# Loading V and V^T one tile pair sooner in a shared DMA queue, and spreading a refill over more steps

## The chip, the cores and the metric

The kernel runs on one core of a Trainium2 chip. The metric is device time in microseconds (us); a smaller one is better. A core has TensorE (PE in the profile; its weight loads are PEld), VectorE (DVE), ScalarE (ACT), GpSimd (POOL) and SyncE (SP), which here issues every DMA. The *granted clock* is the share of TensorE's full clock that its throttle let through (1.00 is all of it).

## The reference

Two independent attention blocks, A and B, forward and backward. For each block with 8 batches of 96 queries, 32 heads, 512 cached keys and a head size of 128:

```python
q = (x @ wq).reshape(B, Sq, H, Dh).transpose(0, 2, 1, 3)
scores = jnp.einsum("bhqd,bhkd->bhqk", q, k_cache) * (Dh ** -0.5)
p = softmax(scores)
o = jnp.einsum("bhqk,bhkd->bhqd", p, v_cache)
out = o.transpose(0, 2, 1, 3).reshape(B, Sq, H * Dh) @ wo
# and, by vjp of the whole with grad_out: dx, dk_cache, dv_cache, dwq, dwo
```

Inputs and outputs are bf16. What matters is the traffic: each cached K and V is read twice (plain, and transposed by the DMA), and each dK and dV is written once. One transfer moves two heads of one batch, 256 KB.

## The kernel before

All work is emitted in *steps* ("ticks"), one for each tile, a (head, batch). Each piece of a tile's work is placed at the tile's step plus an offset, then all pieces are sorted by step and slot. What SyncE issues follows that order strictly. Loads and stores serve a pair of heads, so one pair takes two steps.

```python
OFF = dict(kt=-3, vt=2, vn=1, kn=4, dv=7, dk=10, s2=3, s3=3, s4=4, s5=5, s6=6, s7=8, s8=9)
# kt, vt: transposed loads of K, V   kn, vn: plain loads   dv, dk: stores
# s2: S = Q K^T   s5: O = P V (needs V)   s6: dP = dO V^T (needs V^T)   s8: dQ = dS K (needs K)
...
def p_ldT(h, b, which):          # K^T (5 buffers) or V^T (4 buffers)
    ...
    t_ = kvp.tile([128, F4 * KC, 16], BF16, name=key + "_p", bufs=5 if which == 0 else 4)
    sp(nc.sync.dma_start_transpose(t_[:], src))
def p_ldn(h, b, which):          # K or V (4 buffers each)
    t_ = kvp.tile([128, HP, KC, 128], BF16, name=key, bufs=4)
    sp(nc.sync.dma_start(...))
...
# block B only: x and g are filled again while block A ends and B begins
for t in range(TT):                                   # TT = 6
    tt = tick0 - 11 + 5 * (t // 3)
    em.add(tt - 4, SL_LOAD + 0.5, setup_stage(t))     # staged g tile, in an "ob" buffer
    em.add(tt, SL_HEAD - 1, setup_T(1, t))            # its transposes on PE
for t in range(TT):
    em.add(tick0 + NG0 + t, SL_LOAD + 0.5, setup_nat(1, t, t + 1))       # g, NG0 = 15
    em.add(tick0 + NX0 + 2 * t, SL_LOAD + 0.6, setup_nat(0, t, t + 1))   # x, NX0 = 18
...
# for the first head of each pair, ct the step of the pair
em.add(ct + OFF["vt"], SLOTS["LOAD"], p_ldT(h, b, 1))
em.add(ct + OFF["vn"], SLOTS["LOAD"] + 0.1, p_ldn(h, b, 1))
em.add(ct + OFF["kn"], SLOTS["LOAD"] + 0.1, p_ldn(h, b, 0))
em.add(ct + OFF["dv"], SLOTS["LOAD"] + 0.2, p_st(h, b, 1))
em.add(ct + OFF["dk"], SLOTS["LOAD"] + 0.2, p_st(h, b, 0))
```

Of the kernel before, what the change touches and what calls it, by code (L numbers as in the profile page):

```python
# [30 lines left out]
SL_LOAD = 0  # L31
# [9 lines left out]
SL_GRP = 95  # L41
SL_SETUP = 96

OFF = dict(kt=-3, vt=2, vn=1, kn=4, dv=7, dk=10, s2=3, s3=3, s4=4, s5=5, s6=6, s7=8, s8=9)
HP = 2
HK = [
    dict(pA=-12, pB=-7, pC0=[-6, -4], pC1=[-5, -3], pD1=-2, pD0=0, qA0=21, qA1=25, qB=[28, 25]),
# [7 lines left out]
GT0, NG0, NX0 = 0, 15, 18  # L55
# [4 lines left out]
SLOTS = dict(LOAD=0, S2A=5, S2B=5.5, S7=10, S8=20, S6=25, S5=30, S4=40, S3A=52, S3B=53, S5B=54, HEAD=SL_HEAD, GRP=SL_GRP)  # L60
# [17 lines left out]
def build_block(tc, em, tick0, blk, x, kc, vc, wq, wo, g_all, out_all, dx, dk, dv, dwq, dwo, ident, ones, pools, HG=4, first=True, groups=None):  # L78
# [51 lines left out]
    def setup_nat(which_, t0_, t1_):  # L130
        def f():
            key, _, src_flat = KEYS[which_]
            if t0_ == 0:
                S[key] = const.tile([128, TT, D], BF16, name=key, bufs=1)
            sp(nc.sync.dma_start(S[key][:, t0_:t1_, :], src_flat[t0_ * 128:t1_ * 128, :].rearrange("(t p) d -> p t d", p=128)))
        return f

    def setup_stage(t):
        def f():
            S[("g_nat", t)] = wk.tile([128, D], BF16, name="ob", bufs=4)  # L140
            sp(nc.sync.dma_start(S[("g_nat", t)][:], g_flat[t * 128:(t + 1) * 128, :]))
        return f

    def setup_xT(c):
        def f():
            if c == 0:
                S["xT"] = const.tile([128, DC, T], BF16, name="xT", bufs=1)
            sp(nc.sync.dma_start_transpose(S["xT"][:, c, :], x_flat[:, c * 128:(c + 1) * 128]))
        return f
# [27 lines left out]
    if first:  # L177
        for t in range(TT):
            late = t * 128 >= tsplits[0][1]
            em.add(tick0 - 15, SL_LOAD + (2 if late else 0), setup_nat(0, t, t + 1))  # L180
            em.add(tick0 - (7 if late else 9), SL_HEAD, setup_T(0, t))
            em.add(tick0 + GT0, SL_LOAD - 2, setup_nat(1, t, t + 1))
            em.add(tick0 + GT0, SL_HEAD + (2 if late else -1), setup_T(1, t))
    else:
        for c in range(DC):
            em.add(tick0 - 17 + (3 * c) // 2, SL_LOAD + 0.5, setup_xT(c))
        for t in range(TT):
            tt = tick0 - 11 + 5 * (t // 3)
            em.add(tt - 4, SL_LOAD + 0.5, setup_stage(t))
            em.add(tt, SL_HEAD - 1, setup_T(1, t))  # L190
        for t in range(TT):
            em.add(tick0 + NG0 + t, SL_LOAD + 0.5, setup_nat(1, t, t + 1))
            em.add(tick0 + NX0 + 2 * t, SL_LOAD + 0.6, setup_nat(0, t, t + 1))

    def pA_wq(h):
        def f():
# [75 lines left out]
    def p_ldT(h, b, which):  # L272
        def f():
            key = "KT" if which == 0 else "VT"
            t_ = kvp.tile([128, F4 * KC, 16], BF16, name=key + "_p", bufs=5 if which == 0 else 4)
            src = (kc if which == 0 else vc)[b, h:h + HP].rearrange("h (r f) d -> (h r) (f d)", r=R8)
            sp(nc.sync.dma_start_transpose(t_[:], src))
            for j in range(HP):
                half = t_[:, :, j * R8:(j + 1) * R8]
                CS.setdefault((blk, h + j, b), {})[key] = half.rearrange("p (f c) r -> p f c r", c=KC)  # L280
        return f

    def p_ldn(h, b, which):
        def f():
            key = "K_sb" if which == 0 else "V_sb"
            t_ = kvp.tile([128, HP, KC, 128], BF16, name=key, bufs=4)
            src = (kc if which == 0 else vc)[b, h:h + HP]
            sp(nc.sync.dma_start(t_[:].rearrange("p h c d -> p h (c d)"), src.rearrange("h (p c) d -> p h (c d)", c=KC)))
            for j in range(HP):
                CS[(blk, h + j, b)][key] = t_[:, j]  # L290
        return f
# [229 lines left out]
    def gW(g):  # L521
        def f():
            if g == 0:
                setup_acc()
        return f
# [32 lines left out]
    for g in range(NG):  # L558
        h0 = GH0[g]
        for hh in range(groups[g]):  # L560
            h = h0 + hh
            j = h % HP
            c0t = tick0 + (h - j) * B
            hk = (HKE if first and h >= H - HP else HK if h >= HP else HK1 if first else HK2)[j]
            early = first and h < HP
            soon = 2 if first and HP <= h < 2 * HP and j == 0 else 0
            if j == 0:
                em.add(tick0 - 15 if early else c0t + hk["pA"] + soon, SL_LOAD + (1 if early else 0), pA_wq(h))
            em.add(tick0 + GT0 if early else c0t + hk["pA"] + soon, SL_LOAD - 1 if early else SL_LOAD, pA(h))
            em.add(c0t + hk["pB"], SL_HEAD, pB(h))  # L570
            em.add(c0t + OFF["s5"], SL_LOAD, h_alloc(h))
            for si in range(NTS):
                em.add(c0t + hk["pC0"][min(si, len(hk["pC0"]) - 1)], SL_HEAD, pC(h, 0, si))
                em.add(c0t + hk["pC1"][min(si, len(hk["pC1"]) - 1)], SL_HEAD, pC(h, 1, si))
            em.add(c0t + hk["pD1"], SL_HEAD, pD(h, 1))
            em.add(c0t + hk["pD0"], SL_HEAD, pD(h, 0))
            for b in range(B):
                ct = c0t + b * HP + j
                if j == 0:
                    em.add(tick0 - 13 if early and b == 0 else ct + (max(OFF["kt"], -1) if early else OFF["kt"]), SLOTS["LOAD"], p_ldT(h, b, 0))  # L580
                    em.add(ct + OFF["vt"], SLOTS["LOAD"], p_ldT(h, b, 1))
                    em.add(ct + OFF["vn"], SLOTS["LOAD"] + 0.1, p_ldn(h, b, 1))
                    em.add(ct + OFF["kn"], SLOTS["LOAD"] + 0.1, p_ldn(h, b, 0))
                    em.add(ct + OFF["dv"], SLOTS["LOAD"] + 0.2, p_st(h, b, 1))
                    em.add(ct + OFF["dk"], SLOTS["LOAD"] + 0.2, p_st(h, b, 0))
                em.add(ct + OFF["s2"], SLOTS["S2A"], c_s2a(h, b))
                em.add(ct + OFF["s2"], SLOTS["S2B"], c_s2b(h, b))
                em.add(ct + OFF["s3"], SLOTS["S3A"], c_s3a(h, b))
                em.add(ct + OFF["s3"], SLOTS["S3B"], c_s3b(h, b))
                em.add(ct + OFF["s5"], SLOTS["S5B"], c_s5b(h, b))  # L590
                em.add(ct + OFF["s4"], SLOTS["S4"], c_s4(h, b))
                S45.setdefault(ct + OFF["s5"], [None, None, None])[0] = (blk, h, b)
                S45.setdefault(ct + OFF["s4"], [None, None, None])[1] = (blk, h, b)
                S45.setdefault(ct + OFF["s6"], [None, None, None])[2] = (blk, h, b)
                S78.setdefault(ct + OFF["s8"], [None, None])[0] = (blk, h, b)
                S78.setdefault(ct + OFF["s7"], [None, None])[1] = (blk, h, b)
                em.add(ct + OFF["s6"], SLOTS["S6"], c_s6(h, b))
                em.add(ct + OFF["s7"], SLOTS["S7"], c_s7(h, b))
            em.add(c0t + hk["qA0"], SL_HEAD, qA(h, 0))
            for di in range(len(dsplits)):  # L600
                em.add(c0t + hk["qB"][min(di, len(hk["qB"]) - 1)], SL_HEAD + 1, qB(h, di))
            em.add(c0t + max(hk["qB"]) + (1 if first and h >= H - 3 * HP else 2), SL_LOAD + 0.3, qB_st(h))
            em.add(c0t + hk["qA1"], SL_HEAD, qA(h, 1))
            if j == HP - 1:
                for (k_, c_lo, c_hi) in hk["qD"]:
                    em.add(c0t + k_, SL_HEAD + 2, qD(h - j, c_lo, min(c_hi, DC)))
                em.add(c0t + k_ + 2, SL_LOAD + 0.3, qD_st(h - j))
        cLg = tick0 + (h0 + groups[g]) * B - 1
        gs0 = max(3, (GSPREAD0 * groups[g]) // HG)
        gs1 = max(3, (GSPREAD1 * groups[g]) // HG)  # L610
        em.add(cLg + OFF["s5"] - 2, SL_LOAD, gW(g))
        subs = [(t, di) for t in range(TT) for di in range(len(dsplits))]
        n = len(subs)
        for which in (0, 1):
            for i, (t, di) in enumerate(subs):
                if which == 0:
                    tk = cLg + OFF["s5"] + 2 + (i * gs0) // n
                else:
                    tk = cLg + OFF["s8"] + 2 + gs0 - 3 + (i * gs1) // n
                em.add(tk, SL_GRP, gU(g, which, t, di))  # L620
                if g == NG - 1 and di == len(dsplits) - 1:
                    em.add(tk + 2, SL_LOAD + 0.3, gU_st(g, which, t))
# [124 lines left out]
```

## Time and profile before

| kernel before | |
|---|---|
| time, median of 3 runs | 1647.15 us (1645.1 to 1650.86) |
| profiled execution | 1644.9 us, granted clock 0.998 |
| PE idle in it | 44.2 us (an upper bound, see the result) |
| DMA queue | 454.57 MB, packets' time 103.3% of 16 engines (the packets' times are added up, so this can pass 100%) |

The prediction shows the busy line, the waits and the stages. Here is one more place, the worst in block A. It is the timeline of PE in the kernel before; columns are start, duration, engine, source line, operation, output and inputs, count, and in brackets the idle time just before and what ended it:

```profile
69.62 0.42 PE L411 MATMUL dP_ps<-VT_p,dOT_h 128*96 128x512 bf16 x1 [2.28 <-DMA VT_p<-in_A_v_cache_dram]
...
71.66 0.34 PE L430 MATMUL dq_dst_ps<-dST_sb,K_sb 128*128 128x96 bf16 x4 [0.59 <-DMA K_sb<-in_A_k_cache_dram]
...
74.08 0.50 PE L362 MATMUL optp_ps<-PT_sb,V_sb 128*128 128x96 bf16 x4 [1.41 <-DMA V_sb<-in_A_v_cache_dram]
```

### The profile page before, as it was taken

Reading aid. Unit: us, or ns where it says so; the run is one execution under the profiler, and the core shown is the slowest. Engines: PE = TensorE matmul, PEld = TensorE weight load, DVE = VectorE, ACT = ScalarE, POOL = GpSimd, SP = SyncE. Lnnn points to the kernel's source line nnn. Section 1 sums busy time; section 2 is a strip of 40 time slices with the busy share of each in tenths; the row PEclk is TensorE's granted clock in tenths of the full one; section 3 lists DMA queues with packets and bytes.
Section 4 is the critical chain, followed back from the end, with each engine's and each line's share of the span. In section 5 each row is a group of like instructions: output and inputs, shape, how many; then the busy total and the mean of one; then the engine's idle time right before and its main releaser. Section 6 shows DMA issues by size and latency. Waiting matters only on the chain.

```text
span 1644.9 us, 55391 instructions
## 1 busy us (share of the span) xinstructions
PE 1600.7 (97%) x20713; PEld 1260.4 (77%) x20906; DVE 1340.4 (81%) x3406; ACT 1349.3 (82%) x3498; POOL 533.3 (32%) x1026
## 2 busy tenths in 40 slices
PE   8899999999999999999899999999999999999998
PEld 6777877777777787777777777777787777878776
DVE  5786888888888888878778778888888888888796
ACT  6888988889788798888868889788798888879783
POOL 1333333333333333333323333333333333333331
PEclk9999999999999999999999999999999999999999
DMA  9999999999999999999999999999999999999995
GB/s 263 250 279 283 275 275 288 266 280 287 284 281 288 293 266 287 267 289 270 287 282 297 291 284 288 286 283 291 278 290 273 289 277 297 279 295 271 279 279 170
DMA packets 375566, 458.12 MB, mean 279 GB/s; under 512 B 40704, under 2 KB 367104, under 8 KB 367104
## 3 DMA queue, kind: packets, MB, share of 16 engines
q1 hardware_dynamic: 375296, 454.57, 103.3%
q8 instruction: 163, 2.67, 0.7%
q14 instruction: 107, 0.88, 0.1%
HBM read 160.10 MB, written 159.12 MB: 194 GB/s over the span
## 4 chain that ended last, share of the span: by engine, by line
PE 88%; DMA 6%; ACT 2%; DVE 2%; issue 1%; POOL 0%; SPq 0%; DVEq 0%; ACTq 0%
PE o_ps L536 12%; PE q_ps L250 12%; PE dwq_ps L511 6%; PE dV_ps L387 6%; PE dK_ps L453 6%; PE S_ps L314 6%; PE dwo_ps L491 6%; PE dP_ps L411 6%; PE optp_ps L362 6%; PE optp_ps L369 5%; PE dq_dst_ps L430 5%; PE dq_dst_ps L437 5%; PE n_ps L265 3%; PE nat_ps L477 3%; DMA V_sb<-in_A_v_cache_dram 2%; DMA V_sb<-in_B_v_cache_dram 1%
## 5 line engine op out<-in xcount | busy, mean ns | idle before, releaser
L401 POOL TENSOR_TENSOR prod<-OT_h,dOT_h 128x96 bf16<-128x96 bf16 x512 | 187.4, 366 | 836.0 <-DVE rinv L336 463.3
L346 POOL TENSOR_SCALAR P_sb<-E_sb,rinv 96x512 bf16<-96x512 bf16 x508 | 350.8, 691 | 244.6 <-DVE rinv L336 244.4
L458 ACT ACTIVATE dK_sb<-dK_ps 128x512 bf16<-128x512 f32 x512 | 305.8, 597 | 137.9 <-PE dK_ps L453 135.0
L326 ACT ACTIVATE E_sb<-S_ps,negm 96x512 bf16<-96x512 f32 x512 | 351.9, 687 | 67.0 <-DVE negm L316 53.7
L316 DVE TENSOR_REDUCE negm<-S_ps 96x1 f32<-96x512 f32 x512 | 347.5, 679 | 67.9 <-PE S_ps L314 67.2
L415 DVE SCALAR_TENSOR_TENSOR dS_sb<-dP_ps,dl_ps,P_sb 96x512 bf16<-96x512 f32 x512 | 380.3, 743 | 4.0 <-PE dl_ps L413 3.8
L392 ACT ACTIVATE dV_sb<-dV_ps 128x512 bf16<-128x512 f32 x512 | 307.8, 601 | 12.4 <-PE dV_ps L387 11.0
L376 ACT ACTIVATE PT_sb<-optp_ps 128x384 bf16<-128x384 bf16 x512 | 255.7, 499 | 5.6 <-DVE OT_h L373 4.7
L439 DVE COPY dST_sb<-dq_dst_ps 128x384 bf16<-128x384 bf16 x512 | 177.3, 346 | 50.7 <-PE dq_dst_ps L437 49.2
L411 PE MATMUL dP_ps<-VT_p,dOT_h 128*96 128x512 bf16 x512 | 195.9, 383 | 7.0 <-DMA VT_p<-in_A_v_cache_dram 3.9
L387 PE MATMUL dV_ps<-dOnat_h,P_sb 96*128 96x128 bf16 x2048 | 199.7, 219 | 2.1 <-DVE ob L546 1.7
L453 PE MATMUL dK_ps<-Qnat_h,dS_sb 96*128 96x128 bf16 x2048 | 198.9, 219 | 0.1
L314 PE MATMUL S_ps<-KT_p,QT_h 128*96 128x512 bf16 x512 | 194.0, 379 | 0.3
L453 PEld LDWEIGHTS <-dS_sb 96*128 96x128 bf16 x2048 | 147.5, 97 | 48.0
L362 PE MATMUL optp_ps<-PT_sb,V_sb 128*128 128x96 bf16 x2048 | 169.6, 204 | 10.2 <-DMA V_sb<-in_A_v_cache_dram 5.8
L369 PE MATMUL optp_ps<-ident,P_sb 96*128 96x96 bf16 x2048 | 172.4, 206 | 2.3 <-DVE P_sb L346 1.6
L430 PE MATMUL dq_dst_ps<-dST_sb,K_sb 128*128 128x96 bf16 x2048 | 171.8, 205 | 0.8 <-DMA K_sb<-in_A_k_cache_dram 0.6
L437 PE MATMUL dq_dst_ps<-ident,dS_sb 96*128 96x96 bf16 x2048 | 171.7, 205 | 0.0
L362 PEld LDWEIGHTS <-V_sb 128*128 128x128 bf16 x2048 | 107.0, 96 | 58.8 <-DMA V_sb<-in_A_v_cache_dram 7.9
L536 PE MATMUL o_ps<-wo_r,OT_h 128*128 128x128 bf16 (+1 forms) x722 | 144.5, 294 | 2.4
L536 PE MATMUL o_ps<-wqT_h,dQT_h 128*128 128x512 bf16 (+1 forms) x720 | 144.2, 294 | 2.5
L373 DVE CAST OT_h<-optp_ps 128x96 bf16<-128x96 f32 x512 | 125.0, 244 | 10.9 <-PE optp_ps L369 10.0
(75 smaller groups left out, 3047.4 us busy)
## 6 DMA issues: line engine op xcount, KB each, us to landing
out_dram<-dV_sb SPq DMA_DIRECT2D x256, 256.0 KB, 4.5
out_dram<-dK_sb SPq DMA_DIRECT2D x256, 256.0 KB, 4.4
V_sb<-in_A_v_cache_dram SPq DMA_DIRECT2D x128, 256.0 KB, 4.3
K_sb<-in_A_k_cache_dram SPq DMA_DIRECT2D x128, 256.0 KB, 4.6
V_sb<-in_B_v_cache_dram SPq DMA_DIRECT2D x128, 256.0 KB, 4.3
K_sb<-in_B_k_cache_dram SPq DMA_DIRECT2D x128, 256.0 KB, 4.3
out_dram<-ob SPq DMA_DIRECT2D x88, 160.0 KB, 4.2
out_dram<-wq_p SPq DMA_DIRECT2D x32, 320.0 KB, 5.1
```

The source lines that it names most:

```text
L314: nc.tensor.matmul(S_ps[:], hs["QT_h"][:, tok], st["KT"], start=True, stop=True)
L316: nc.vector.tensor_reduce(negm[:], S_ps[:], axis=AX.X, op=ALU.max, negate=True)
L326: nc.scalar.activation(E_sb[:].rearrange("q (a f) -> q a f", f=F4), st["S_ps"][:].rearrange("q (f a) -> q a f", f=F4), ACT.Exp, bias=st["n ...
L346: eng.tensor_scalar(P_sb[:], st["E_sb"][:], st["rinv"][:], 0.0, op0=ALU.mult, op1=ALU.add)
L362: nc.tensor.matmul(OT_ps, st["V_sb"][:, c, :], st["PT_sb"][:, c * Sq:(c + 1) * Sq], start=(c == 0), stop=(c == KC - 1))
L387: nc.tensor.matmul(dV_ps[:, c * 128:(c + 1) * 128], P_sb[:, c * 128:(c + 1) * 128], hs["dOnat_h"][:, b * 128:(b + 1) * 128], start=True, s ...
L392: nc.scalar.activation(dV_p[:, j], dV_ps[:], ACT.Identity, scale=1.0)
L411: nc.tensor.matmul(dP_ps[:], hs["dOT_h"][:, tok], st["VT"], start=True, stop=True)
L415: nc.vector.scalar_tensor_tensor(dS_sb[:].rearrange("q (a f) -> q a f", f=F4), dP_ps[:].rearrange("q (f a) -> q a f", f=F4), dl_ps[:, 0:1] ...
L453: nc.tensor.matmul(dK_ps[:, c * 128:(c + 1) * 128], dS_sb[:, c * 128:(c + 1) * 128], hs["Qnat_h"][:, b * 128:(b + 1) * 128], start=True, s ...
L458: nc.scalar.activation(dK_p[:, j], dK_ps[:], ACT.Identity, scale=1.0)
L536: nc.tensor.matmul(o_ps[:], src[:, t * 128:(t + 1) * 128], rhs, start=(hh == 0), stop=(hh == groups[g] - 1))
```

## The change

Its intent: V and V^T have the least lead from load to use (four steps), so they get two more. The refill of x and g, which crowds the queue at the block boundary, is spread over 20 steps in place of 14, and the second half of the staged g tiles gets two more steps before PE needs it. Whole but for its context lines:

```diff
-OFF = dict(kt=-3, vt=2, vn=1, kn=4, dv=7, ...)
+OFF = dict(kt=-3, vt=0, vn=-1, kn=4, dv=7, ...)
-            tt = tick0 - 11 + 5 * (t // 3)
-            em.add(tt - 4, SL_LOAD + 0.5, setup_stage(t))
+            tt = tick0 - 11 + 7 * (t // 3)
+            em.add(tick0 - 15 + 5 * (t // 3), SL_LOAD + 0.5, setup_stage(t))
             em.add(tt, SL_HEAD - 1, setup_T(1, t))
-            em.add(tick0 + NG0 + t, SL_LOAD + 0.5, setup_nat(1, t, t + 1))
-            em.add(tick0 + NX0 + 2 * t, SL_LOAD + 0.6, setup_nat(0, t, t + 1))
+            em.add(tick0 + NG0 - 1 + 2 * t, SL_LOAD + 0.5, setup_nat(1, t, t + 1))
+            em.add(tick0 + NX0 + 3 * t, SL_LOAD + 0.6, setup_nat(0, t, t + 1))
-                    em.add(ct + OFF["vt"], ..., p_ldT(h, b, 1))
-                    em.add(ct + OFF["vn"], ..., p_ldn(h, b, 1))
+                    em.add(max(ct + OFF["vt"], tick0 + 2) if early else ct + OFF["vt"], ..., p_ldT(h, b, 1))
+                    em.add(max(ct + OFF["vn"], tick0 + 1) if early else ct + OFF["vn"], ..., p_ldn(h, b, 1))
```

More of the change, by code (lines that the diff above doesn't have):

```diff
@@ L42 @@
 SL_SETUP = 96
-OFF = dict(kt=-3, vt=2, vn=1, kn=4, dv=7, dk=10, s2=3, s3=3, s4=4, s5=5, s6=6, s7=8, s8=9)
+OFF = dict(kt=-3, vt=0, vn=-1, kn=4, dv=7, dk=10, s2=3, s3=3, s4=4, s5=5, s6=6, s7=8, s8=9)
 HP = 2
@@ L580, in build_block @@
                     em.add(tick0 - 13 if early and b == 0 else ct + (max(OFF["kt"], -1) if early else OFF["kt"]), SLOTS["LOAD"], p_ldT(h, b, 0))
-                    em.add(ct + OFF["vt"], SLOTS["LOAD"], p_ldT(h, b, 1))
-                    em.add(ct + OFF["vn"], SLOTS["LOAD"] + 0.1, p_ldn(h, b, 1))
+                    em.add(max(ct + OFF["vt"], tick0 + 2) if early else ct + OFF["vt"], SLOTS["LOAD"], p_ldT(h, b, 1))
+                    em.add(max(ct + OFF["vn"], tick0 + 1) if early else ct + OFF["vn"], SLOTS["LOAD"] + 0.1, p_ldn(h, b, 1))
                     em.add(ct + OFF["kn"], SLOTS["LOAD"] + 0.1, p_ldn(h, b, 0))
```

## The prediction

> **What bounds the kernel now.** I read the page first: the busy line, the slices, the DMA rows.
>
> ```profile
> PE 1600.7 (97%) x20713; PEld 1260.4 (77%) x20906; DVE 1340.4 (81%) x3406; ACT 1349.3 (82%) x3498; POOL 533.3 (32%) x1026
> ...
> DMA  9999999999999999999999999999999999999995
> ...
> q1 hardware_dynamic: 375296, 454.57, 103.3%
> ```
>
> TensorE (PE) is idle for only 1644.9 - 1600.7 = 44.2 us, and the DMA row is full in every slice but the last. So two things are near their limit at once: PE sets the end, and the queue of transfers that feeds it has hardly a free moment. Next, PE's waits, to see what a better load order could win:
>
> ```profile
> PE optp_ps L362 <- DMA V_sb<-in_A_v_cache_dram: 5.8, 6, 2.0
> PE dP_ps L411 <- DMA VT_p<-in_A_v_cache_dram: 3.9, 2, 2.3
> PE optp_ps L362 <- DMA V_sb<-in_B_v_cache_dram: 3.0, 5, 1.0
> PE dP_ps L411 <- DMA VT_p<-in_B_v_cache_dram: 2.3, 1, 2.3
> PE tp_ps L159 <- DMA ob<-in_grad_out_dram: 2.2, 1, 2.2
> ...
> PE dq_dst_ps L430 <- DMA K_sb<-in_A_k_cache_dram: 0.6, 1, 0.6
> ```
>
> Waits on V and V^T are 5.8 + 3.9 + 3.0 + 2.3 = 15.0 us, those on the staged g tiles 2.2; together 17.2 us, 1.0% of the time. That is all that the change can aim at directly. K is waited for once. Where they lie, by stage (windows; columns: stretch, length, busy time of PE, PEld, DVE, ACT, POOL, clock, DMA share, GB/s):
>
> ```profile
> 400.00:760.00 360.00, 357.01 (x4655) 281.86 (x4699) 303.08 (x774) 299.79 (x780) 121.14 (x232) 1.00 1.05 282
> 760.00:800.00 40.00, 35.81 (x469) 28.08 (x471) 29.87 (x76) 30.15 (x78) 11.64 (x23) 1.00 1.01 270
> ...
> 880.00:930.00 50.00, 43.57 (x580) 34.06 (x583) 38.21 (x97) 41.33 (x109) 16.60 (x32) 1.00 1.04 294
> 930.00:1600.00 670.00, 665.24 (x8676) 525.23 (x8755) 559.44 (x1429) 564.47 (x1471) 225.64 (x431) 1.00 1.06 283
> ```
>
> PE is 99% busy in the long stretches (357.01 of 360, 665.24 of 670). The block boundary (760 to 930) is one bad place. The timeline shows the other, around 70 us: PE waits there 2.28 us for V^T, 0.59 for K and 1.41 for V within 7 us, and the windows of 2 us show the granted clock at 0.50 from 72 to 78, about 3 us more.
>
> Last, the DMA queue in one pair of steps (SyncE's timeline; start, duration), because every transfer goes through it in order:
>
> ```profile
> 1444.42 1.18 SPq L277 DMA_TRANSPOSE KT_p<-in_B_k_cache_dram  x1
> 1445.70 0.53 SPq L288 DMA_DIRECT2D V_sb<-in_B_v_cache_dram  x1
> 1446.35 0.39 SPq L297 DMA_DIRECT2D out_dram<-dV_sb  x1
> 1446.84 1.17 SPq L277 DMA_TRANSPOSE VT_p<-in_B_v_cache_dram  x1
> 1448.43 0.39 SPq L288 DMA_DIRECT2D K_sb<-in_B_k_cache_dram  x1
> 1448.92 0.40 SPq L297 DMA_DIRECT2D out_dram<-dK_sb  x1
> 1449.38 2.08 SPq L277 DMA_TRANSPOSE KT_p<-in_B_k_cache_dram  x1
> ```
>
> Six transfers in 4.96 us, one after the other, while a pair of steps takes PE 2 x (1608.3 - 16.2) / 511 = 6.23 us (first and last start of the 512 S products). The wq, wo, dwo and dwq transfers fill most of the rest. SyncE issues nearly without a pause.
>
> **What the Trainium skill says.** "DMA: Bandwidth & Descriptors", section "Issuing engines are not separate DMA queues", says that all DMAs run on the same 16 engines and interleave; the 103.3% and the full row agree. So a V load moved forward moves another transfer back; it adds no bandwidth. The same page's "Rules for kernel authors" says to issue a DMA early and wait on its semaphore late. The trace agrees where it hurts: V lands 4.3 us (median) after its issue, and at 305.78 us it was issued only some 4.4 us before PE wanted it, so PE lost 2.0 us. "Perfetto Trace Analysis", section "What "DMA-bound" means", names an issuing sequencer that is solid DMA slices as one way to be DMA-bound; the SyncE rows above come close. "TensorE: Matmul & The Clock Gate", Part 1, says that an idle window of about 3.4 us halves the clock; the 0.50 after the stalls at 67 to 74 us fits.
>
> **The change, part by part.** No instruction or byte is added. *V and V^T, vt 2 to 0, vn 1 to -1.* A pair of tiles takes two steps, so the order of kinds in the queue stays, and V and V^T belong to the pair one further on. In the DMA order of the two compiled programs, V and V^T loads stand four to six places earlier, and, what matters as much, every K^T and K load two places later from the third pair on. In steps from load to use: V 4 becomes 6, V^T 4 becomes 6, K stays 5, K^T 6.
>
> I took each load's landing from the trace and subtracted it from the first product that uses it (the slack). At the stalls V and V^T have 0. They gain one pair (6.23 us) less two transfers of about 1 us, so some 4 us: enough for every stall listed, the longest being 2.3. By itself this gives 15.0 us. But PE may come forward only as far as the next stream allows, and that is K, whose landing the reorder does not improve. Its slack at the bad places: 0.05 us at the K load of 65.5 us, 1.36 at 116, 2.6 at 216, 1.29 at 317, 1.67 at 417, 2.3 at 771, 1.0 at 886, 2.1 to 2.9 from 900 to 919, 2.7 at 931. If the queue is really full, K's landings stay where they are or come up to 2 us later, and PE's lead over the old run is capped by these numbers whatever V does:
> - Around 70 us: K lands at 71.66 as before or a little later. The 2.28 us wait for V^T becomes a wait for K of about 3 us or more; V's 1.41 after it can go. Worth 0 to 1.4 us; the half clock stays as likely as not.
> - 80 to 760 us: V waits of 0.43, 1.61 and 2.01 us go, but the K slack of 1.3 us at 317 caps the lead there. I count 1 us.
> - From 930 us on there is no V wait to remove; V's slack was growing to about 10 us by the end.
>
> *Staged g tiles.* The transposes of tiles 3 to 5 come two steps later behind the same loads. The 2.18 us wait at 783.6 is before this batch if it is the first, and is cured if it is the second; its loads went out at 779.28, 4.3 us before, and it is the second (the first was issued at 757.5 and used at 764.7). Saving 2.2 us, capped by K's 2.3 to 2.5 us: with the V^T wait at 796 (1.61 us), about 1 to 2 us net.
>
> *Refill of x and g, spread to twice the steps.* Twelve transfers of 160 KB, some 0.3 to 0.5 us each in the queue, come over 20 steps instead of 14. Beside the first K loads after 880 us one or two fewer refills stand ahead, so K^T and K lose their two places there: 0.5 to 1 us more K slack. Of the 0.37 + 1.03 + 0.89 + 0.46 + 2.29 us of V waits listed between 887 and 924 (5.0), K's 1.0 to 2.9 us lets through about 2 us.
>
> Sum: 0.5 + 1 + 1.5 + 2 = 5 us at best if the caps add; as the lead is carried, the caps do not add where the queue stays full. I take 4 us: 1647 - 4 = 1643.
>
> **Rivals.** (1) *The queue has air and all 15 to 17 us come out:* 1631, or 1628 if the half clock at 72 us goes too. For it: K is waited for once, for 0.6 us, and its median slack is several us. Against: the DMA row, and K's slack of 0 to 2 us at just the places where V's is 0. (2) *The queue is the bound and nothing comes out:* V waits turn into K waits of the same length, 1647. For it: K's slack of 0.05 at 70 us and 1.0 at 886. (3) *It gets worse:* with four V buffers, V's reuse now follows its last reader by one step instead of three, so SyncE can stand behind PE and hold up K and the stores behind it: 1650 to 1655. Against: SyncE runs 1 to 3 steps behind PE in block A (V at 305.78 goes out in the step before its use, three steps after its place), so the buffer is long free. In block B it runs level with PE, but there V, K and K^T have 6 to 12 us of slack. (4) *The later g transposes delay the first projections of block B:* they still stand three steps before their first reader; a us or none.
>
> **Range and chances.** 1643 us. The three runs before span 1645.1 to 1650.9, so 3 us of either side is noise in a median. Full success of rival 1 is at the low side and rival 3 at the high side; eight in ten I give to 1634 to 1650. Two per cent would be 33 us, twice what PE waits for on all these loads together: faster by over 2% 0.01, within 2% 0.98, slower by over 2% 0.01.
>
> **What would show it.** Right: waits of L362 and L411 on V and V^T near 0 (from 15.0 us), the g wait gone, and a new group of L430 waits on K of several us, the largest near 70 us and 885 to 930 us; PE's idle time falls from 44 by less than 8 us; DMA share still over 100%. Wrong, if the V waits go and no K waits come, and PE's idle time falls by 12 us or more: then the queue had air. Wrong the other way, if SyncE's L288 and L277 rows grow by waits for PE, or if V waits stay.

## The result, and the profile after

The changed kernel took 1643.3 us (median of 4 runs, 1641.78 to 1644.22), the kernel before 1649.01 us in the same comparison. The ratio is 0.9967, 95% interval 0.9943 to 0.999. Ratios here are the mean time of one kernel's fast runs over that of the other's fast runs of the same rounds, so not quite the ratio of the medians quoted.

Because executions of one kernel spread over some 10 us, I timed the changed kernel twice more. The three ratios are 0.9967, 0.9993 and 0.9979, all below 1; two of the three intervals exclude 1, and the plain mean is 0.998. The gain is about 0.2%, some 3 us.

Waits of PE in the changed kernel's profile (columns: engine, tile and line, what it waited for, us in total, times, longest):

```profile
PE dq_dst_ps L430 <- DMA K_sb<-in_A_k_cache_dram: 11.4, 8, 3.4
PE dwo_ps L491 <- DMA g_nat<-in_grad_out_dram: 2.5, 1, 2.5
PE dwq_ps L511 <- DMA x_nat<-in_B_x_dram: 1.8, 1, 1.8
```

Every wait for V, V^T and the staged g tiles is gone; they made 17.2 us. In their place stand K, 0.6 us before and 11.4 now, and two waits that the kernel before did not have at all, on the refilled g and x. The waits for loads that the two tables show sum to 17.8 us before (15.0 + 2.2 + 0.6) and 15.7 after; with the small ones that they leave out (x_nat and wq_p at the start, K^T) 18.9 and 17.8. The span fell by 2.5 us, from 1644.9 to 1642.4. One trace of each kernel can't tie the two together, as executions of one kernel differ by more than that.

PE's idle time fell from 44.2 to 42.9 us. Both are too high: these two traces hold 20713 PE records for 20906 weight loads, so 193 matmuls are missing. A later trace of the changed kernel that has all 20906 (`after_third`) shows 28.7 us.

The stages of the changed kernel (columns as in the prediction):

```profile
400.00:760.00 360.00, 356.92 (x4647) 281.58 (x4690) 303.15 (x776) 300.14 (x780) 121.31 (x232) 1.00 1.06 283
760.00:800.00 40.00, 36.20 (x476) 28.53 (x479) 29.53 (x74) 30.69 (x79) 11.96 (x23) 1.00 1.04 256
800.00:880.00 80.00, 74.63 (x952) 58.82 (x960) 62.29 (x158) 59.99 (x154) 23.27 (x45) 1.00 1.06 296
880.00:930.00 50.00, 45.05 (x607) 35.92 (x611) 39.34 (x100) 41.92 (x111) 17.53 (x34) 1.00 1.05 296
```

Of the kernel before, the row that the prediction leaves out:

```profile
800.00:880.00 80.00, 77.06 (x981) 60.53 (x989) 63.97 (x161) 61.92 (x159) 24.11 (x46) 1.00 1.06 289
```

The long stretch is as before (PE 356.92 us busy, 357.01 before). Between 880 and 930 us PE gained 1.5 us of busy time (45.05 against 43.57), between 760 and 800 only 0.4, and between 800 and 880 it lost 2.4 (74.63 against 77.06): over the whole boundary nothing is gained. Part of such differences is work that moved across the edge of a window. The DMA share stays above 1.0. And the place around 70 us, in the changed kernel's PE timeline:

```profile
61.25 0.34 PE L430 MATMUL dq_dst_ps<-dST_sb,K_sb 128*128 128x96 bf16 x4 [2.41 <-DMA K_sb<-in_A_k_cache_dram]
...
74.08 0.50 PE L430 MATMUL dq_dst_ps<-dST_sb,K_sb 128*128 128x96 bf16 x4 [3.45 <-DMA K_sb<-in_A_k_cache_dram]
```

Before, V^T, K and V cost 2.28 + 0.59 + 1.41 = 4.28 us here. Now K alone costs 2.41 + 3.45 = 5.86. The same lateness came out at the next stream in the queue. The granted clock fell to 0.50 at both waits (windows of 2 us show it at 64 to 66 and 74 to 78 us).

### The profile page after: what moved, and what is told of

It reads as the page before. It is cut to its first block, busy times and chain, and to the rows that moved or that the text cites. A ratio compares the mean times of both kernels' runs of the same rounds, so it can differ in the third digit from the quotient of the medians.

```text
span 1642.4 us, 55143 instructions
## 1 busy us (share of the span) xinstructions
PE 1599.5 (97%) x20713; PEld 1261.2 (77%) x20906; DVE 1339.0 (82%) x3406; ACT 1349.3 (82%) x3498; POOL 534.5 (33%) x1026
## 3 DMA queue, kind: packets, MB, share of 16 engines
q1 hardware_dynamic: 375296, 454.57, 103.4%
## 4 chain that ended last, share of the span: by engine, by line
PE 89%; DMA 5%; ACT 3%; issue 1%; DVE 1%; SPq 0%; POOL 0%; DVEq 0%; ACTq 0%
PE o_ps L536 12%; PE q_ps L250 12%; PE dV_ps L387 6%; PE dK_ps L453 6%; PE dwq_ps L511 6%; PE S_ps L314 6%; PE dP_ps L411 6%; PE dwo_ps L491 6%; PE optp_ps L362 6%; PE optp_ps L369 5%; PE dq_dst_ps L430 5%; PE dq_dst_ps L437 5%; PE n_ps L265 3%; PE nat_ps L477 3%; DMA K_sb<-in_A_k_cache_dram 2%
## 5 line engine op out<-in xcount | busy, mean ns | idle before, releaser
L430 PE MATMUL dq_dst_ps<-dST_sb,K_sb 128*128 128x96 bf16 x2048 | 172.2, 206 | 12.0 <-DMA K_sb<-in_A_k_cache_dram 11.4
L430 PEld LDWEIGHTS <-K_sb 128*128 128x128 bf16 x2048 | 122.9, 97 | 14.1 <-DMA K_sb<-in_A_k_cache_dram 13.3
```

Of the source, the lines that this page charges most:

```text
L430: nc.tensor.matmul(dQT_ps, st["K_sb"][:, c, :], st["dST_sb"][:, c * Sq:(c + 1) * Sq], start=(c == 0), stop=(c == KC - 1))
```

## The experiments

The theory: the queue is full, so a load that moves forward pushes others back, and PE's wait passes to the stream with the next least lead. First the change is taken apart, then the theory's causes are tried one at a time. All kernels were timed over five rounds against the kernel before; in each group of runs named together they share its runs. Medians of different groups should not be compared, as the kernel before itself moved from 1641 to 1650 us between groups.

**V and V^T alone** (`e1_v_only`), **refill and staged tiles alone** (`e2_refill_stage_only`), **V, V^T and staged tiles** (`e3_v_and_stage`).

```diff
# e1: the changed kernel, with
-            tt = tick0 - 11 + 7 * (t // 3)                 # and the refill
+            tt = tick0 - 11 + 5 * (t // 3)                 # as before
# e2: the kernel before, with only the changed lines of refill and staged tiles
# e3: the changed kernel, with the refill as before
```

> Only the V and V^T loads move (vt 0, vn -1); refill of x and g and the staged g tiles as before. Theory (the transfer queue is full, V's wait is exchanged for a shorter K wait): waits of L362 and L411 on V and V^T below 1 us (15.0 before), waits of L430 on K 6 to 12 us, no wait on the refilled g_nat or x_nat; ratio to before 0.995 to 0.999. Rival A (the gain of the changed kernel is the spread refill's): V waits between 880 and 930 us stay at 2 us or more and the ratio is 0.999 to 1.001. Rival B (the spread refill costs what the shift wins at the boundary): this one is faster than the whole change, ratio 0.993 to 0.996.

> Only the spread refill of x and g and the two later steps for the staged g tiles; V and V^T loads as before. Theory: the V and V^T waits of block A (9.7 us before) stay, those after 880 us (5.3 us) shrink by less than half, the g wait at 783 us goes (2.2 us), and waits on g_nat at L491 or x_nat at L511 of 1 to 4 us may appear, as in the changed kernel (2.5 and 1.8 us); ratio 0.998 to 1.001. Rival A (the refill is what wins): V waits after 880 us go to 0 and the ratio is 0.995 to 0.998.

> The changed kernel with the refill of x and g put back to its old steps. Theory: the waits on g_nat (2.5 us) and x_nat (1.8 us) that the changed kernel shows are gone; K waits at 880 to 930 us come up by 0 to 2 us, because the refills stand closer together in front of K; ratio 0.994 to 0.997, that is level with the whole change (0.9967) or up to 3 us faster. Rival (the spread refill is needed once V loads come sooner): K or V waits of over 4 us between 880 and 930 us and a ratio of 0.998 or more.

Measured: V alone 1645.35 us, ratio 0.9993 (0.9969 to 1.0017); refill and staged tiles alone 1643.18 us, 0.998 (0.9958 to 1.0001); V and staged tiles 1644.79 us, 0.9994 (0.9971 to 1.0018); before 1646.65. Which part holds the 0.2% these ratios cannot tell. The waits can tell more. V alone:

```profile
PE dq_dst_ps L430 <- DMA K_sb<-in_A_k_cache_dram: 6.8, 5, 2.4
PE tp_ps L159 <- DMA ob<-in_grad_out_dram: 3.2, 1, 3.2
PE dq_dst_ps L430 <- DMA K_sb<-in_B_k_cache_dram: 2.1, 3, 0.9
```

The moved loads alone turn all V and V^T waits (15.0 us) into 8.9 us of K waits, as expected; the wait for staged g (3.2 us) stays, as it should, and there is none for the refilled g or x. The ratio is just above the 0.995 to 0.999 that was expected. Refill and staged tiles alone:

```profile
PE optp_ps L362 <- DMA V_sb<-in_A_v_cache_dram: 6.1, 3, 2.7
PE optp_ps L362 <- DMA V_sb<-in_B_v_cache_dram: 2.2, 4, 1.3
...
PE dwo_ps L491 <- DMA g_nat<-in_grad_out_dram: 1.8, 1, 1.8
```

The spread refill brings the g wait with it (1.8 us), and V waits between 870 and 935 us become 2.2 + 1.1 (V^T) = 3.3 us, 5.3 before. So the spread refill gives back as a refill wait most of what it takes from V. In `e3`, without it, no wait for the refilled g or x is left; K waits sum to 21.0 us, only 2.4 of them between 880 and 930 (0 to 2 were expected). Its ratio missed: 0.994 to 0.997 was expected, and 0.9994 is where the rival put it, without the 4 us of waits that the rival asked for. Rival B of the first run (V alone clearly faster than the whole) was not borne out: no difference among these kernels is clear of noise.

**K one step sooner as well** (`e4_k_one_step`), in the same group.

```diff
# e3, and
-OFF = dict(kt=-3, vt=0, vn=-1, kn=4, ...
+OFF = dict(kt=-3, vt=0, vn=-1, kn=3, ...
```

> As the run before it in this list, and the K loads one step sooner too (kn 3 in place of 4), no buffer added. Theory: K has the least lead once V and V^T have moved, so K waits fall from about 11 us to 2 to 5 us and the ratio to before is 0.990 to 0.994 (some 1633 to 1639 us). Rival (the queue's rate sets the pace of block A, lead does not matter): the waits move to K^T at L314 or to ACT's dV_sb and dK_sb (buffers waiting for stores) with the same sum, ratio 0.995 to 0.998. Rival 2 (SyncE stands behind PE for the K buffer, which its last reader frees one step before): SyncE's L288 rows grow and the ratio is over 0.998.

Measured: 1668.29 us, ratio 1.0133 (1.011 to 1.0156). I expected a gain of 8 us or more and got a loss of 22. K waits did vanish. ACT's waits in this kernel show where the time went instead:

```profile
ACT dV_sb L392 <- DMA out_dram<-dV_sb: 34.0, 34, 4.0
```

ACT writes dV into one of four buffers and must wait until the store of four pairs ago has landed. So the stores had become the last in the queue. That sum is larger than the loss of 22 us, and it did not settle the cause: either the lead taken from the stores cost this, or the queue had become slower. One thing in its order was new. SyncE's sequence in a pair had been transpose, copy, copy, transpose, copy, copy; with K on the other step it was transpose, copy, copy, copy, transpose, copy. The next group separates the two. (Rival 2, SyncE standing before K's buffer, doesn't explain it: SyncE's waits for PE at L288 did grow, from 111.7 us in `e3` to 184.9, but the kernel before has 219.0 there and is fast.)

**K two steps sooner, order kept** (`e5_k_two_steps`), **V and V^T by one step only** (`e6_v_one_step`), **only V one step later** (`e9_v_other_step`), and **the changed kernel again** (`after_again`).

```diff
# e5: e3, and
-    kn=4;  K^T 5 buffers, K 4 buffers
+    kn=2;  K^T 4 buffers, K 5 buffers      # order: transpose, copy, copy, transpose, copy, copy
# e6: the changed kernel, and
-OFF = dict(kt=-3, vt=0, vn=-1, ...
+OFF = dict(kt=-3, vt=1, vn=0, ...          # transpose, transpose, four copies
# e9: the changed kernel, and
-OFF = dict(kt=-3, vt=0, vn=-1, ...
+OFF = dict(kt=-3, vt=0, vn=0, ...          # transpose, copy, transpose, three copies
```

> V, V^T (two steps) and K (two steps, with five K buffers and four K^T buffers in place of four and five) all one pair sooner; refill as before; staged tiles as in the change. The queue keeps its pattern of one transpose and two copies, unlike the run with K one step sooner, where two transposes had one copy between them. Theory P (that pattern cost the 22 us, by leaving the DMA engines short): ratio 0.995 to 1.001 here, time with fewer than 16 packets in flight back near 2% of the time; K waits under 4 us, and a new wait of ACT for dV_sb on its store of 5 to 15 us, because in a full queue the stores now have the least lead. Rival L (sooner K loads push the stores back, ACT waits for dV_sb, and that cost the 22 us): ACT waits on dV_sb of 30 us or more and a ratio of 1.008 or more here too.

> The changed kernel with V and V^T moved by one step only (vt 1, vn 0): two transposes directly after one another, then four copies. K keeps its place. Theory P (the order of transposes and copies matters): ratio 1.005 to 1.02, DMA share of the long stretches under 1.05. Rival L (only lead matters): V's lead of five steps equals K's, K and V waits together 8 to 16 us as in the changed kernel, ratio 0.995 to 1.001.

> The changed kernel with only the V load one step later (vn 0, vt 0): the same pattern as in the run with K one step sooner (transpose, copy, transpose, three copies), but K is not moved and V keeps a lead of five steps. Theory P: ratio 1.005 to 1.015 as there, with ACT waits for dV_sb or K waits of over 20 us. Rival L: no ACT wait on dV_sb over 5 us, ratio 0.995 to 1.001.

> The changed kernel again, unedited, to see how firm its ratio of 0.9967 is: four runs of before have by now spread from 1640 to 1651 us. Theory (V waits exchanged for shorter K waits, a gain of a few us): ratio 0.995 to 0.999, profile with K waits of 8 to 16 us and refill waits of 2 to 5 us. Rival (the 5.5 us were the luck of four runs): ratio 0.9985 to 1.002.

| | median us | ratio | 95% interval |
|---|---|---|---|
| kernel before | 1648.11 | | |
| changed kernel again | 1646.51 | 0.9993 | 0.9968 to 1.0018 |
| K two steps sooner, order kept | 1649.62 | 1.0011 | 0.9986 to 1.0036 |
| V one step later | 1682.03 | 1.021 | 1.0181 to 1.0239 |
| V and V^T one step only | 1764.24 | 1.07 | 1.0671 to 1.0728 |

The order of transposes and copies decides. Moving K by two steps and keeping the order costs nothing that these runs can tell from noise; a shift of V or of V and V^T by one step costs 2.1% and 7.0%, although it changes neither bytes nor the number of transfers. Less lead is not the cause: in `e6` V and V^T lead by five steps, between the four of the kernel before and the six of the changed one. Nor is it an uneven load of the steps: `e6`, the slowest, has three transfers in each step, as the kernel before. `e6` and `e9` overshot what I expected of theory P (up to 1.02 and 1.015). The stretch 930 to 1600 us in `e6`, `e9` and `e5`, in this order, a fence each:

```profile
930.00:1600.00 670.00, 630.11 (x8046) 492.42 (x8119) 523.17 (x1318) 529.87 (x1375) 209.51 (x402) 0.98 0.99 262
```

```profile
930.00:1600.00 670.00, 655.09 (x8493) 515.42 (x8569) 547.33 (x1386) 556.26 (x1449) 219.84 (x422) 1.00 1.03 276
```

```profile
930.00:1600.00 670.00, 665.31 (x8668) 525.41 (x8748) 559.44 (x1425) 563.54 (x1470) 224.83 (x431) 1.00 1.06 284
```

Read the last two columns: the DMA share is 1.06 with the order kept (`e5`), 1.03 in `e9` and 0.99 in `e6`, the rate 284, 276 and 262 GB/s, while PE waits more. The queue moves less in a microsecond although loads are late. The timeline of SyncE in `e6` shows what stands in front of them:

```profile
1245.06 1.14 SPq L277 DMA_TRANSPOSE VT_p<-in_B_v_cache_dram  x1
1246.25 1.63 SPq L277 DMA_TRANSPOSE KT_p<-in_B_k_cache_dram  x1
1247.98 0.53 SPq L297 DMA_DIRECT2D out_dram<-dV_sb  x1
```

Two transposes one after the other keep SyncE for 2.9 us until the next copy can go. Over the trace from 100 to 1590 us, a transpose issued right after a transpose holds SyncE 2.25 us in the mean (221 of them), one after a store 1.50 us in the changed kernel (463). Averaged over all transfers of that stretch, SyncE holds 0.89 us for each in `e6` and 0.83 in the changed kernel, and is 91% busy in both. Why a transpose after a transpose takes longer, and whether it is SyncE's issuing or the DMA engines that hold it, no view shows, and I leave it open.

`e5` answers the other half. With K two steps sooner no K wait is left, but ACT's waits for dV stores, 5.3 us in its base `e3`, have doubled:

```profile
ACT dV_sb L392 <- DMA out_dram<-dV_sb: 10.8, 11, 2.1
```

So `e3`'s 21.0 us of K waits are gone, stores land later for ACT, and the time is no better. Lead that is given to one stream in a full queue is taken from another. Rival L, which wanted 30 us or more of this wait and a ratio of 1.008, falls; so most of the 22 us of the run with K one step sooner is most likely the order's (`e5` also has one K buffer more and one K^T buffer less). That each of its 34 us of store waits follows from the slower queue alone I have not shown. The packets in flight, of which the expectation speaks, no view on record shows.

`after_again` missed: its ratio, 0.9993, lies in the range of the rival (the 5.5 us were the luck of four runs), and its K waits, 17.1 and 3.7 us in a profiled execution of 1655.7 us, are above the 8 to 16 expected. The three traces of the changed kernel have 8.9 us of K waits at a span of 1638.3 us, 11.4 at 1642.4 and 20.8 at 1655.7: longer executions have longer K waits, some 12 of the 17 us between the first and the last. What makes the queue lag more in one execution than in another is not shown. The spread is larger than the gain under study.

**Half of the dV stores left out**, in the changed order (`e7_half_dv`) and in the old one (`e10_before_half_dv`), and **dV stores issued by GpSimd** (`e8_dv_from_pool`). The first two give a wrong dV on purpose; all other outputs were right.

```diff
# e7, e10: in p_st, for dV
-            sp(nc.sync.dma_start(dst[...], t_[:]))              # two heads
+            sp(nc.sync.dma_start(dst[...][:, 0:1], t_[:, 0:1])) # first head alone
# e8: in p_st, for dV
-            sp(nc.sync.dma_start(...))
+            nc.gpsimd.dma_start(...)
```

> The changed kernel storing only the first head of each dV pair (dV is wrong on purpose; 128 KB less of 1.5 MB in each pair of steps, same number of transfers). Theory (a full queue is what PE waits for, not the order): K waits fall from 11 to 21 us to below 4 us, no other wait on a load takes their place, PE idle time falls by 10 us or more, ratio 0.985 to 0.993. Rival (the waits are the loads' own latency or SyncE's issuing, as many instructions as before): K waits stay at 8 us or more, ratio 0.996 to 1.0.

> The kernel before with the same half of the dV stores left out (dV wrong on purpose). Theory: with air in the queue the order hardly matters: V and V^T waits fall from 15 us to below 5 us with the old order, and the time is within 0.3% of the run above. Rival (the V loads were issued too late whatever the queue does): V waits stay at 10 us or more and it is 0.5% or more slower than the run above.

> The changed kernel with all 256 dV stores issued by GpSimd in place of SyncE; the bytes are the same. If the 16 DMA engines are the limit: K waits of 8 us or more stay, ratio 0.995 to 1.005. If SyncE's issuing is the limit (six issues of 4.96 us in a pair of 6.23 us): K waits below 4 us, ratio 0.99 to 0.995. Third way: SyncE's transposes now have one copy between them and GpSimd's P tiles are held up by the issuing: ratio over 1.01, with PE waits on P_sb or prod.

Measured against 1649.9 us: changed order with half dV 1633.47 us, ratio 0.991 (0.9892 to 0.9928); old order with half dV 1630.93 us, 0.9896 (0.9878 to 0.9914). The largest wait for a load left in each, changed order first:

```profile
PE dq_dst_ps L433 <- DMA K_sb<-in_A_k_cache_dram: 2.0, 4, 0.9
```

```profile
PE optp_ps L365 <- DMA V_sb<-in_B_v_cache_dram: 3.9, 5, 1.8
```

(The edit moves the lines by three.) SyncE issues as many transfers as before; only 128 KB of the 1.5 MB of a pair are missing. A half store is no quicker to issue: it holds SyncE 0.50 us in the mean, a whole one 0.47 in the changed kernel (100 to 1590 us). K waits fall to 2.0 us, and with the old, late V loads the waits for V and V^T fall from 15.0 to 5.0 (3.9 in the line shown, and 0.6 and 0.5). PE's idle time is 17.7 us in `e7`, 11.0 less than in `after_third`, the trace of the changed kernel with as complete records. The two times lie 0.2% apart with overlapping intervals. So it is the amount that the DMA engines have to move which made PE wait (bytes fall by 7.4%, packets by 8.7%; which of the two counts is not separated), and with less to move V's lead no longer matters. That is the theory's strongest test, and it holds. These runs also give an estimate of what the change could have won at most: about 1%.

The share of the DMA engines does not show that air:

```profile
q1 hardware_dynamic: 342528, 421.02, 99.9%
```

That is `e7`, with 2.0 us of K waits; the changed kernel has 103.4%, and `e6`, 7% slower, 96.8%. A share near 100% does not tell by itself whether loads come too late.

With GpSimd issuing the dV stores: 1675.26 us, ratio 1.0162 (1.014 to 1.0183), the third way that was foreseen.

```profile
PE dl_ps L416 <- POOL prod L404: 22.3, 30, 1.5
PE optp_ps L372 <- POOL P_sb L349: 9.4, 18, 1.5
```

GpSimd's busy time rose from 534.5 to 721.7 us, and PE waited for its tiles. SyncE's transposes also stood closer together here, with one copy between some. So this run does not tell SyncE's issuing from the engines' work; the half stores do.

**The changed kernel a third time** (`after_third`), alone.

> The changed kernel a third time, unedited, because the first two ratios, 0.9967 and 0.9993, leave open whether it gains at all. Theory (in a full queue V waits become K waits, and what is left of the gain is about a tenth of a per cent): ratio 0.997 to 1.0. Rival (a real gain of a third of a per cent): ratio below 0.997. Profile: no V or V^T wait over 0.5 us, K waits of 8 us or more.

Measured: 1637.97 us against 1640.96, ratio 0.9979 (0.9963 to 0.9995). Its profile has 8.9 us of K waits and 2.6 us for the refilled g, none on V. A gain of about 0.2%, not of a third of a per cent.

No version beats both kernels clear of noise and with right results.

## Why the prediction was right

The mechanism was right: a full queue, and V's waits exchanged for K's. The 1643 us rest on a sum of capped savings. The caps were the right idea, but the single terms were not, and that their sum fits is luck.

*What bounds it.* Full queue beside a nearly full PE: confirmed by the half stores (0.991 and 0.9896 with the same instructions issued).

*V and V^T waits go, K waits come.* Foreseen as near 0, and "L430 waits on K of several us"; measured 0 and 11.4 us, in three traces of the changed kernel 8.9 to 20.8. Of the places foreseen for the largest, 70 us was right; between 885 and 930 us no trace of the changed kernel has a K wait, and the refill's waits stand there. PE's idle time fell by 1.3 us, where less than 8 was foreseen. Rival 1 (all 15 to 17 us come out) fell. Rival 2 (nothing comes out) is off by some 0.2% only.

*PE's idle time.* The 44.2 us that the prediction starts from are too high, as matmul records are missing; nothing in its sum rests on them.

*Around 70 us.* I expected a K wait of about 3 us or more and the half clock to stay as likely as not. It was 3.45 us with 2.41 more at 61 us that I had not listed, and the clock fell twice. I had put 0 to 1.4 us as a gain; the waits there grew by 1.6 us. Wrong sign.

*80 to 760 us.* The V waits of 0.43, 1.61 and 2.01 us were to be capped by K's slack at 317 us. K waits of 0.42 and 0.60 us appeared at 309 and 322 us, just there. The place was right, the size was not: all waits for loads of this stretch fell from 4.4 us to 1.0, 3.4 us against the 1 that I counted.

*Staged g.* The 2.2 us wait went. Four K waits of 0.74, 0.72, 1.52 and 1.51 us between 781 and 804 us took its place and that of V^T's 1.61, 4.5 us against 3.8: the term "1 to 2 us net" was too high: 0.7 us were lost.

*Refill.* Here a step was missing. ("Twice the steps" is loose, too: 20 in place of 14.) I counted what fewer refills in front of K would save, and did not ask when the last refilled tile is needed. Spreading them made the sixth g tile 2.5 us and the x tiles 1.8 us late. V's 5.3 us went (5.0 in the prediction's list, which leaves out one of 0.22), 4.3 came back: 0.9 us net against 2.

*The sum.* 0.5 + 1 + 1.5 + 2 = 5, taken as 4; in the waits of these two traces -1.6 + 3.4 - 0.7 + 0.9 = 2.0. Two terms of four had the wrong sign, one was three times too small, one twice too large. The first comparison's 5.7 us between medians is at the high end; over three comparisons the gain is some 3 us. Nor do these terms carry weight singly: K waits alone differ by 12 us among three traces of the changed kernel.

*Range.* It held all medians of the changed kernel: 1643.3, 1646.5, 1638.0. The width of 16 us was needed for the spread of executions alone.

*What the prediction passed over.* It noted that the order of kinds in the queue stays, as a remark. The experiments show that to be the condition for the change to be harmless: the same shift by one step in place of two costs 7.0%.

## What to carry to other kernels

When a queue is as full as this one, sooner loads mostly choose which stream is late (here 15.0 us of V waits became 8.9 to 20.8 of K waits): list every stream's slack from landing to first use, stores' buffers included, and expect the wait at the next smallest. Read a shift of a schedule by the sequence that it leaves in the queue, not only by the lead: in this queue, transposes wanted two copies between them (one between some cost 1.3% and 2.1%, none 7.0%). To test whether a wait is order or amount, leave some bytes out and see if all waits for loads go together. And when a refill is spread to relieve the queue, check its last tile against its first reader.

## What the Trainium skill lacked or had wrong

- "DMA: Bandwidth & Descriptors", section "DMA Transpose (X-bar)", gives constraints and alternatives, but no cost for the order of transposes and copies in one queue. Here two transposes in a row, same bytes and same number of transfers, took the kernel from 1648.11 to 1764.24 us (ratio 1.07), the DMA rate in the long stretch from 284 (with the order kept) to 262 GB/s, and a transpose right after a transpose held SyncE 2.25 us against 1.50 after a store.
- The same page's section "Rules for kernel authors" advises to issue early and wait late. It does not say that this may gain next to nothing in a full queue: V and V^T waits went from 15.0 us to 0, K waits from 0.6 to 11.4, and the time fell by about 0.2%.
- "Perfetto Trace Analysis", section "What "DMA-bound" means", has no test for a trace in which the engines and the issuing sequencer both look near full, as here (103.4%, and SyncE 91% busy between 100 and 1590 us). Leaving out half of one store, with every issue kept, did it: K waits from 11.4 to 2.0 us.
